# Other homes for the MLP tiles in each partition of SBUF

## The chip, the core and the metric

The kernel runs on one core of a Trainium2 chip. The metric is device time in microseconds, from the start to the end of one execution. Three timed runs of the kernel before gave 779.7, 779.81 and 780.31 us; the median is 779.81 us.

## What is computed

An attention whose mask comes from hashed buckets, on two batches of eight heads with 768 tokens and head size 64, and behind it two MLPs on the 1536 tokens of 512 features that it gives:

```
attn: x[b,h] = softmax(where(bucket(q) == bucket(k), q k^T / 8, -1e9)) v
x = transpose of attn to 1536 x 512
h = x @ w_in  (512 x 2048);  g = h - tanh(h);            x = g @ w_out (2048 x 512)
h = x @ w2_in (512 x 2048);  g = h * sigmoid(1.702 h);   out = g @ w2_out
```

The MLP weights arrive as 64-bit floats.

## The kernel before

**Attention** takes the first 257 us. It walks over 96 steps of 128 queries of one head: scores (line 333), softmax, transposes (line 368), product with v (line 387), and it leaves its result as two fp32r parts, xh (rounded) and xl (the rest).

**The MLPs** follow as 16 chunks, 0 to 7 for the first and 8 to 15 for the second. A chunk is two blocks (j = 0, 1) of 128 hidden features, on three blocks (t) of 512 tokens. Every product is made of three fp32r matmuls, high by high, high by low, low by high. A matmul has a stationary operand, 128 x 128, which LDWEIGHTS loads, and a moving operand, 128 x 512, which MATMUL streams past it; in the profile's names, as in `o<-gh,wh`, the moving one stands first. In line 611 (`products`) the stationary operand is a piece of the w_in weights (wh, wl) or of sums of them (sh, sl), and the moving operand is x (xh, xl) or differences of x (th, tl): sh, sl, th and tl come from a scheme that makes eight block products out of seven. In line 700 (`out_mm`) the first MLP has the w_out weights (wh, wl) stationary and the activations (gh, gl) moving. The second MLP has them the other way round: activations stationary, weights moving. In every steady chunk these are 138 matmuls of 512 columns: 72 in line 700 and 66 in line 611.

The other engines feed that. DVE unpacks the 64-bit weights (raw to w, lines 109 to 135), gates (line 664) and adds outputs to the accumulators acc01 and acc2 (line 708). ACT rounds weights, sums and activations to their high parts (lines 141, 566, 668). POOL makes the low parts (lines 144, 570, 673). The order on every engine is written out by hand in the strings STEADY and ORDER; no scheduler changes it.

**Homes.** A tile pool takes its place in the partition when it is entered, one behind the other, and its tiles lie in it in the order in which they are first asked for. The pools of the attention are closed at line 513, and the MLP's pools are laid over the same bytes. So a tile's home follows from the order of the `tile_pool` calls (lines 75 to 77, 90, 173 to 177, 518 to 522) and from the sizes alone. The first 16 KB of a partition are reserved, four small constants stand behind them, and the first tile starts 128 bytes past 16 KB. All further tiles that matter are multiples of 512 bytes, except `ready`, which has 64 bytes: what lies behind `ready` starts at 192 modulo 512.

Of the kernel before, what the change touches and what calls it, by code (L numbers as in the profile page):

```python
# [10 lines left out]
F32 = mybir.dt.float32  # L11
F32R = mybir.dt.float32r
# [15 lines left out]
NCC = DM // 128  # L28
# [6 lines left out]
TB = 512  # L35
# [22 lines left out]
def lsh_attention_then_two_mlps(  # L58
# [15 lines left out]

    xpool = ctx.enter_context(tc.tile_pool(name="xpool", bufs=1))
    wp0 = ctx.enter_context(tc.tile_pool(name="wp0", bufs=1))
    ps = ctx.enter_context(tc.tile_pool(name="ps", bufs=1, space=PSUM))
    ctx.enter_context(tc.manual_schedule())

    xh = xpool.tile([128, NCC, NT], F32R, name="xh")  # L80
    xl = xpool.tile([128, NCC, NT], F32R, name="xl")

    acc01 = xpool.tile([128, NCC, 2 * TB], F32, name="acc01")

    wh = {}
    wl = {}
    todo = {}
    parts = {}
    wpools = [wp0]
    rawp = [ctx.enter_context(tc.tile_pool(name="rawa", bufs=1))]  # L90

# [422 lines left out]


    wpools.append(ctx.enter_context(tc.tile_pool(name="wp1", bufs=1)))
    rawp.append(ctx.enter_context(tc.tile_pool(name="rawm", bufs=1)))
    op = ctx.enter_context(tc.tile_pool(name="op", bufs=1))  # L520
    sp = ctx.enter_context(tc.tile_pool(name="sp", bufs=2))
    gp = ctx.enter_context(tc.tile_pool(name="gp", bufs=1))
    acc2 = op.tile([128, NCC, TB], F32, name="acc2")
    th = op.tile([128, 3, 2, TB], F32R, name="th")
    tl = op.tile([128, 3, 2, TB], F32R, name="tl")


    ready = op.tile([128, 16], F32, name="ready")
# [9 lines left out]
    gh = {}  # L538
    gl = {}
# [107 lines left out]
    def apart(c, t, j):  # L647
        return t == j or t == 2 if c % LAYER else j == 0
# [15 lines left out]
        nc.vector.tensor_tensor(g, h, f, ALU.subtract if c < LAYER else ALU.mult)  # L664

    def g_hi(c, t, j):
        gh[c, t, j] = gp.tile([128, TB], F32R, tag=f"gh{t}{j}", name=f"gh{c}_{t}_{j}")
        nc.scalar.activation(gh[c, t, j], fs[c, t, j], AF.Copy)  # L668

    def g_lo(c, t, j):  # L670
        gl[c, t, j] = gp.tile([128, TB], F32R, tag=f"gl{t}{j}", name=f"gl{c}_{t}_{j}")
        eng = nc.gpsimd if apart(c, t, j) else nc.vector
        eng.tensor_tensor(  # L673
            gl[c, t, j], fs.pop((c, t, j)), gh[c, t, j].bitcast(F32), ALU.subtract
        )
# [79 lines left out]
    def issue(name, c):  # L755
# [12 lines left out]
        elif kind == "ts":  # L768
            t_sum(c, *n)
        elif kind in ("th", "tl"):  # L770
            (t_hi if kind == "th" else t_lo)(*n)
        elif kind == "P":
            product(c, n[0])
        elif kind in ("kp", "ku"):
            keep(c, n[0], yw[c, 0])
        elif kind in ("xadd", "zadd", "wadd"):
            add(c, kind[0])
        elif kind == "h":
            t, j = n
            tag = "T" if c % LAYER or t != 1 else "vg"[j]  # L780
            hp[c, t, j] = bank(tag, f"h{c}_{t}_{j}")
            h_mm(c, t, j, hp[c, t, j])
        elif kind == "t":
            act(c, *n)
        elif kind == "g":
            gate(c, *n)
        elif kind in ("hi", "lo"):
            (g_hi if kind == "hi" else g_lo)(c, *n)
        elif kind == "o":
            out_mm(c, *n)  # L790
        elif kind == "ev":
            evac(c, *n)
        elif kind in ("xh", "xl"):
            (x_hi if kind == "xh" else x_lo)(*n)
        elif kind == "tab":
            nc.scalar.activation(ready, ready, AF.Sigmoid)
# [136 lines left out]
```

## Time and profile before

| | |
|---|---|
| median of three runs | 779.81 us |
| span of the profiled execution | 778.2 us |
| so, outside the span | 1.6 us |
| TensorE busy (PE) | 759.1 us, 98% |
| VectorE busy (DVE) | 582.0 us, 75% |
| ScalarE busy (ACT) | 424.6 us, 55% |
| GpSimd busy (POOL) | 399.4 us, 51% |
| attention | 0 to 257 us |
| first MLP | 257 to about 522 us |
| second MLP | from there to the end |

The profiled execution was recorded once; its span is what all sums are made against, and 1.6 us are added to come to the median. PE's busy time counts overlapping, modelled ends of pipelined matmuls: a single MATMUL is shown as some 390 ns long while the next one starts 227 to 236 ns after it. What counts for the time is the distance from start to start, called pitch here. At the full clock of 2.4 GHz, 512 columns are 213.3 ns.

### The profile page before, as it was taken

The numbers are of one execution on the slowest core, as the hardware profiler recorded it, in microseconds if no ns is written. First come the engines' busy times: TensorE is split into PE (matmuls) and PEld (weight loads), VectorE is DVE, ScalarE is ACT, GpSimd is POOL, SyncE is SP. The second block draws the span as 40 slices with busy tenths as digits, with TensorE's granted clock in tenths as the row PEclk, the third lists the DMA queues.
The fourth block names the chain that finished last, engine by engine and source line by source line (L and its number), as shares of the span: only waits on it lengthen the run. The fifth ranks groups of instructions, "written<-read, shape, count | busy, mean of one in ns | idle before, by whom it ended". The sixth has DMA issues, their size and how long they took to land.

```text
span 778.2 us, 10045 instructions
## 1 busy us (share of the span) xinstructions
PE 759.1 (98%) x3708; PEld 570.3 (73%) x3708; DVE 582.0 (75%) x840; ACT 424.6 (55%) x793; POOL 399.4 (51%) x342
## 2 busy tenths in 40 slices
PE   4899999999999999999999999999999999999997
PEld 2666666666665788888888888887878888888885
DVE  4778778767766768778787788897798778877643
ACT  3777777777777465454353453556545345353430
POOL 6442651652500686474554735799775473554610
PEclk9999999999999999999999999999999999999999
DMA  9536135134010212021131111212112111120004
GB/s 260 178 102 208 70 103 163 57 107 160 25 54 0 109 55 109 34 76 55 54 109 55 54 55 55 108 27 83 55 55 102 61 55 54 55 109 0 1 1 162
DMA packets 12993, 62.89 MB, mean 81 GB/s; under 512 B 1616, under 2 KB 2512, under 8 KB 8848
## 3 DMA queue, kind: packets, MB, share of 16 engines
q1 hardware_dynamic: 8928, 46.21, 16.4%
q0 software_dynamic: 3872, 15.99, 7.2%
q8 instruction: 29, 0.48, 0.3%
q14 instruction: 20, 0.16, 0.1%
q10 hardware_dynamic: 144, 0.05, 0.0%
HBM read 59.10 MB, written 3.15 MB: 80 GB/s over the span
## 4 chain that ended last, share of the span: by engine, by line
PE 88%; DVE 4%; issue 2%; POOL 2%; DMA 2%; ACT 1%; POOLq 0%; DVEq 0%; ACTq 0%
PE o L700 31%; PE h L611 12%; PE y L611 10%; PE pv L387 9%; PE tp L368 9%; PE sc L333 8%; PE w L611 5%; PE x L611 2%; DMA ka<-in_kd 1%; DMA r<-in_rr 1%; POOL xl L723 1%; DVE nm L347 1%; PE rb L412 1%; PE pb L261 1%; PE po L292 1%
## 5 line engine op out<-in xcount | busy, mean ns | idle before, releaser
L673 POOL TENSOR_TENSOR gl<-f,gh 128x512 fp32r<-128x512 f32 x62 | 85.9, 1386 | 170.9 <-ACT gh L668 165.5
L708 DVE TENSOR_TENSOR acc<-o,acc 128x512 f32<-128x512 f32 x168 | 108.8, 684 | 54.4 <-PE o L700 53.6
L376 ACT ACTIVATE pt<-tp 128x384 f32<-128x384 f32 x184 | 80.3, 489 | 47.7 <-PE tp L368 47.1
L347 DVE TENSOR_REDUCE nm<-sc 128x1 f32<-128x768 f32 x96 | 91.5, 954 | 14.6 <-PE sc L333 13.4
L368 PEld LDWEIGHTS tp<-eye_sb,pr 128*128 128x128 f32 x576 | 61.6, 140 | 53.5 <-issue 25.7
L351 ACT ACTIVATE pr<-sc,nb 128x768 f32<-128x768 f32 x96 | 86.9, 905 | 15.8 <-DVE nb L349 8.8
L144 POOL TENSOR_TENSOR wl<-w,wh 128x512 fp32r<-128x512 f32 (+1 forms) x62 | 85.7, 1393 | 19.0 <-ACT wh L141 19.0
L732 ACT ACTIVATE u<-y 128x512 f32<-128x512 f32 x42 | 25.3, 601 | 107.8 <-PE y L611 107.8
L368 PE MATMUL tp<-eye_sb,pr 128*128 128x128 f32 x576 | 83.5, 281 | 0.0
L387 PE MATMUL pv<-pt,v 128*64 128x384 f32 x384 | 82.0, 510 | 0.0
L700 PE MATMUL o<-wh,gh 128*128 128x512 f32 x192 | 76.2, 397 | 0.7 <-ACT acc L706 0.6
L700 PE MATMUL o<-wh,gl 128*128 128x512 f32 x192 | 76.0, 396 | 0.5 <-POOL gl L673 0.5
L700 PE MATMUL o<-wl,gh 128*128 128x512 f32 x192 | 75.9, 395 | 0.0
L700 PE MATMUL o<-gh,wh 128*128 128x512 f32 x192 | 75.9, 395 | 0.0
L700 PE MATMUL o<-gh,wl 128*128 128x512 f32 x192 | 75.4, 393 | 0.0
L700 PE MATMUL o<-gl,wh 128*128 128x512 f32 x192 | 75.3, 392 | 0.0
L611 PE MATMUL h<-xl,wh 128*128 128x512 f32 x160 | 62.6, 391 | 0.3 <-POOL xl L723 0.3
L611 PE MATMUL h<-xh,wh 128*128 128x512 f32 x160 | 62.6, 391 | 0.0
L611 PE MATMUL h<-xh,wl 128*128 128x512 f32 x160 | 62.6, 391 | 0.0
L333 PE MATMUL sc<-ka,qa 128*128 128x384 f32 x192 | 55.8, 372 | 2.4 <-DVE qa L237 1.9
L668 ACT ACTIVATE gh<-f 128x512 fp32r<-128x512 f32 x62 | 39.0, 629 | 28.3 <-DVE f L664 28.1
L333 PE MATMUL sc<-kb,qb 128*128 128x384 f32 x192 | 50.2, 342 | 2.0 <-DVE qb L299 2.0
(138 smaller groups left out, 1652.1 us busy)
## 6 DMA issues: line engine op xcount, KB each, us to landing
raw<-in_w SPq DMA_DIRECT2D x32, 1024.0 KB, 4.8
ka<-in_kd POOLq DMA_DIRECT2D x7, 768.0 KB, 4.6
qa<-in_qd POOLq DMA_DIRECT2D x7, 768.0 KB, 6.8
r<-in_rr SPq DMA_DIRECT2D x7, 768.0 KB, 4.5
v<-in_vv SPq DMA_DIRECT2D x8, 384.0 KB, 3.1
out<-acc SPq DMA_DIRECT2D x12, 256.0 KB, 2.1
qb<-in_qd POOLq DMA_DIRECT2D x7, 384.0 KB, 8.1
r<-in_rr SPq DMA_DIRECT2D x2, 384.0 KB, 4.5
```

The costliest lines, as they stand in the source:

```text
L144: nc.gpsimd.tensor_tensor(wl[c, j][:, f], ws[c, j][:, f], wh[c, j][:, f].bitcast(F32), ALU.subtract)
L333: nc.tensor.matmul(sc[:, hf, :HALF], (qa, qb)[n][:, h, t0 : t0 + QT], (ka, kb)[n][:, h, hf * HALF : (hf + 1) * HALF], start=(n == 0), stop ...
L347: nc.vector.tensor_reduce(nm, sc[:, :, :HALF], AX.XY, ALU.max, negate=True)
L351: nc.scalar.activation(pr.rearrange("p (a b) -> p a b", a=2), sc[:, :, :HALF], AF.Exp, bias=nb, scale=D**-0.5, accum_out=sums[u][:, j, h : ...
L368: nc.tensor.transpose(tp[:, k * 128 : (k + 1) * 128], pr[:, c * 128 : (c + 1) * 128], eye_sb)
L376: nc.scalar.activation(dst, src, AF.Copy)
L387: nc.tensor.matmul(acc[u][h * 64 : (h + 1) * 64, :UT], v[:, h, c, :], probT[u][:, c, h, :], start=(c == 0), stop=(c == NCH - 1),)
L611: nc.tensor.matmul(o, a, b, start=(start and n == 0 and m == 0), stop=(n == len(pairs) - 1 and m == 2), skip_group_check=not start,)
L668: nc.scalar.activation(gh[c, t, j], fs[c, t, j], AF.Copy)
L673: eng.tensor_tensor(gl[c, t, j], fs.pop((c, t, j)), gh[c, t, j].bitcast(F32), ALU.subtract)
L700: nc.tensor.matmul(o, a, m, start=(first and n == 0), stop=(not first and n == 2))
L708: nc.vector.tensor_tensor(m, o, m, ALU.add)
```

## The change

Seven pools change place; not one instruction is added, removed or moved. On each of the five engines the built programs stand in the same order, instruction for instruction. acc01 goes to a pool of its own (apool) on the right-hand side, that is, at the far end of the partition, and the first block's raw and w buffers (rawa) go there too. th and tl get a pool of their own (tp) directly behind the weights; sh and sl (sp) and gh and gl (new pool ghl) follow, then u and f (gp), then acc2 and `ready` (op), and the second block's raw and w buffers (rawm) come last.

```diff
     xpool = ctx.enter_context(tc.tile_pool(name="xpool", bufs=1))
     wp0 = ctx.enter_context(tc.tile_pool(name="wp0", bufs=1))
+    apool = ctx.enter_context(tc.tile_pool(name="apool", bufs=1, side="right"))
...
-    acc01 = xpool.tile([128, NCC, 2 * TB], F32, name="acc01")
+    acc01 = apool.tile([128, NCC, 2 * TB], F32, name="acc01")
...
-    rawp = [ctx.enter_context(tc.tile_pool(name="rawa", bufs=1))]
+    rawp = [ctx.enter_context(tc.tile_pool(name="rawa", bufs=1, side="right"))]
...
     wpools.append(ctx.enter_context(tc.tile_pool(name="wp1", bufs=1)))
+    tp = ctx.enter_context(tc.tile_pool(name="tp", bufs=1))
+    sp = ctx.enter_context(tc.tile_pool(name="sp", bufs=2))
+    ghl = ctx.enter_context(tc.tile_pool(name="ghl", bufs=1))
+    gp = ctx.enter_context(tc.tile_pool(name="gp", bufs=1))
+    op = ctx.enter_context(tc.tile_pool(name="op", bufs=1))
     rawp.append(ctx.enter_context(tc.tile_pool(name="rawm", bufs=1)))
-    op = ctx.enter_context(tc.tile_pool(name="op", bufs=1))
-    sp = ctx.enter_context(tc.tile_pool(name="sp", bufs=2))
-    gp = ctx.enter_context(tc.tile_pool(name="gp", bufs=1))
+    th = tp.tile([128, 3, 2, TB], F32R, name="th")
+    tl = tp.tile([128, 3, 2, TB], F32R, name="tl")
     acc2 = op.tile([128, NCC, TB], F32, name="acc2")
-    th = op.tile([128, 3, 2, TB], F32R, name="th")
-    tl = op.tile([128, 3, 2, TB], F32R, name="tl")
...
-        gh[c, t, j] = gp.tile([128, TB], F32R, tag=f"gh{t}{j}", name=f"gh{c}_{t}_{j}")
+        gh[c, t, j] = ghl.tile([128, TB], F32R, tag=f"gh{t}{j}", name=f"gh{c}_{t}_{j}")
...
-        gl[c, t, j] = gp.tile([128, TB], F32R, tag=f"gl{t}{j}", name=f"gl{c}_{t}_{j}")
+        gl[c, t, j] = ghl.tile([128, TB], F32R, tag=f"gl{t}{j}", name=f"gl{c}_{t}_{j}")
```

The homes, in KB from the start of a partition, with the start modulo 512 bytes, as the two built programs have them:

| tiles | read by TensorE as | before | after |
|---|---|---|---|
| xh, xl | moving | 16 to 64, 128 | the same |
| wh, wl, even chunks | stationary; moving in the second MLP's line 700 | 80 to 96, 128 | 64 to 80, 128 |
| wh, wl, odd chunks | the same | 108 to 124, 128 | 80 to 96, 128 |
| th, tl | moving | 144 to 168, 128 | 96 to 120, 128 |
| sh, sl | stationary | 168 to 184, 192 | 120 to 136, 128 |
| gh, gl | moving in the first MLP, stationary in the second | 198 to 222, 192 | 136 to 160, 128 |
| u, f | not read | 184 to 198, 192 | 160 to 174, 128 |
| acc2 | not read | 136 to 144, 128 | 174 to 182, 128 |
| raw, w of j = 1 | not read | 124 to 136, 128 | 182 to 194, 192 |
| raw, w of j = 0 | not read | 96 to 108, 128 | 196 to 208, 480 |
| acc01 | not read | 64 to 80, 128 | 208 to 224, 480 |
| attention: qa, qb | stationary | 111 to 135, 128 | 83 to 107, 128 |
| attention: ka, kb | moving | 135 to 159, 128 | 107 to 131, 128 |
| attention: v | stationary | 165 to 171, 128 | 137 to 143, 128 |
| attention: pr | stationary | 171 to 180, 128 | 143 to 152, 128 |
| attention: pt | moving | 180 to 216, 128 | 152 to 188, 128 |

Because the MLP's homes overlap other attention tiles than before, a dozen waits at the seam between attention and MLP differ; all others are the same. The one that starts a transfer later is that of raw1_1, the first load of chunk 1's second block: before, it waits for the last matmul of the attention; after, also for POOL's last piece of the attention (line 436).

## Rows read from the trace of the kernel before

**Rows 1.** The page: busy time by engine, PE's granted clock in 40 slices.
```profile
PE 759.1 (98%) x3708; PEld 570.3 (73%) x3708; DVE 582.0 (75%) x840; ACT 424.6 (55%) x793; POOL 399.4 (51%) x342
...
PEclk9999999999999999999999999999999999999999
```

**Rows 2.** The page: chain of work that ended last, by engine.
```profile
PE 88%; DVE 4%; issue 2%; POOL 2%; DMA 2%; ACT 1%; POOLq 0%; DVEq 0%; ACTq 0%
```

**Rows 3.** PE from 257 us, instructions in order: start us, us, what.
```profile
259.99 0.39 PE L611 MATMUL h<-xh,wh 128*128 128x512 f32 x1
...
267.93 0.39 PE L611 MATMUL h<-xh,wl 128*128 128x512 f32 x1
268.15 0.40 PE L700 MATMUL o<-gh,wh 128*128 128x512 f32 x1
268.39 0.40 PE L700 MATMUL o<-gl,wh 128*128 128x512 f32 x1
```

**Rows 4.** PE in chunk 11 of the second MLP, the same view.
```profile
641.75 0.40 PE L700 MATMUL o<-wh,gh 128*128 128x512 f32 x1
641.99 0.39 PE L700 MATMUL o<-wl,gh 128*128 128x512 f32 x1
...
644.55 0.40 PE L611 MATMUL y<-th,sh 128*128 128x512 f32 x1
```

**Rows 5.** The chain in order of time, merged: start us, us, what xcount.
```profile
366.63 5.51 PE o L700 x24
...
398.42 5.51 PE o L700 x24
...
601.57 5.60 PE o L700 x24
...
633.57 5.60 PE o L700 x24
```

**Rows 6.** PE in the attention at 202 us, scores of 384 columns.
```profile
202.25 0.51 PE L333 MATMUL sc<-ka,qa 128*128 128x384 f32 x2
202.60 0.51 PE L333 MATMUL sc<-kb,qb 128*128 128x384 f32 x2
```

**Rows 7.** The chain in order of time, from 500 to 575 us.
```profile
506.57 1.29 DVE acc L708 x2
...
537.03 1.67 PE o L700 x6
```

**Rows 8.** PE's two longest waits in the MLPs: us in total, times, longest.
```profile
PE o L700 <- ACT acc L706: 0.6, 1, 0.6
PE o L700 <- POOL gl L673: 0.5, 1, 0.5
```

**Rows 9.** One steady chunk: us, busy by engine (instructions), PEclk, DMA share, GB/s.
```profile
602.00:634.00 32.00, 32.00 (x140) 25.93 (x139) 24.83 (x34) 14.16 (x22) 16.79 (x15) 1.00 0.18 66
```

**Rows 10.** Groups by line: busy us, mean ns | idle before, releaser.
```profile
L708 DVE TENSOR_TENSOR acc<-o,acc 128x512 f32<-128x512 f32 x168 | 108.8, 684 | 54.4 <-PE o L700 53.6
...
L368 PE MATMUL tp<-eye_sb,pr 128*128 128x128 f32 x576 | 83.5, 281 | 0.0
L387 PE MATMUL pv<-pt,v 128*64 128x384 f32 x384 | 82.0, 510 | 0.0
...
L126 DVE SCALAR_TENSOR_TENSOR w<-raw,w 128x1024 uint32<-128x1024 uint32 x32 | 42.3, 1322 | 0.4
...
L591 DVE TENSOR_TENSOR acc<-acc 128x512 f32<-128x512 f32 x4 | 6.3, 1568 | 0.8 <-POOL xl L723 0.6 <-issue 0.2
```

**Rows 11.** The seam: SP's queue, POOL and DVE in order of time.
```profile
257.27 0.80 SPq L103 DMA_DIRECT2D raw<-in_w  x2
...
258.50 1.34 POOL L436 TENSOR_TENSOR xl<-xs,xh 128x384 fp32r<-128x384 f32 x1
...
269.43 1.80 DVE L109 TENSOR_SCALAR raw<-raw 128x1024 f32<-128x1024 f32 x1
```

**Rows 12.** The raw tiles from 225 to 300 us: issue to landing.
```profile
DMA to landing us min/median/max: 4.7/4.8/6.8
```

## The prediction, made before the changed kernel had run

> **What bounds the kernel now.** I read the shares of the engines first. TensorE is busy for 98% of the span, and the chain of work that ended last is PE for 88% [rows 1, 2]; its granted clock is 1.00 in every slice, that is, 2.4 GHz. In the MLPs its matmuls waited for other engines for little more than a microsecond in its longest waits [rows 8], and in a steady chunk it is busy for all of 32.00 us while DVE, the next, has 24.8 [rows 9]. So time can come only from the matmuls' own pace, and the next view is the list of matmuls in order of time, from start to start.
>
> There the pace is not one. From 259.99 to 268.15 us, 36 starts of line 611 with xh, xl moving and wh, wl stationary stand 8.16 / 36 = 226.7 ns apart, which is 213.3 ns of columns at 2.4 GHz and 13.3 ns more [rows 3]. The first matmul that streams gh, at 268.15, is 0.24 us long instead of 0.22 or 0.23, on the same weights. In the second MLP 12 matmuls with gh and gl stationary take 641.75 to 644.55, 2.80 / 12 = 233.3 ns each, on the same columns and at the same clock [rows 4]. Nothing waits in between.
>
> What tells the two kinds apart in the table of homes: the quick ones read only tiles between 16 and 124 KB that start at 128 modulo 512; the slow ones read at least one tile that lies between 168 and 222 KB and starts at 192 modulo 512. In before these two marks go together, so the trace can't say which is the cause. The change removes both from everything that TensorE reads in the MLPs.
>
> **The change, part by part.** *The pace.* A steady chunk is 138 matmuls. In the first MLP one chunk lasts from 366.63 to 398.42, 31.79 us or 230.4 ns a matmul; in the second from 601.57 to 633.57, 32.00 us or 231.9 ns [rows 5]. At 226.7 ns a chunk is 31.28 us. That is 0.51 us (1.6%) less in the first MLP and 0.72 us (2.25%) in the second. The first counts from 257 to 506.6 us, where the chain leaves PE [rows 7]: 249.4 x 1.6% = 4.0 us. The second counts from 537.0, where the chain is back on PE [rows 7], to about 770: 233 x 2.25% = 5.2 us. Between 506.6 and 537 the chain runs over DVE, POOL and ACT, which make the second MLP's input; there a quicker PE only waits longer, and I count nothing. For stops of PE that grow when it is quicker I take off 0.3 us, about a quarter of the 1.1 us that rows 8 have now. Sum: 4.0 + 5.2 - 0.3 = 8.9 us.
>
> Is 226.7 ns the right pace for the new homes? Weights at 64 to 96 KB and th, tl at 96 to 120 lie inside the range that is quick now. The activations at 136 to 160 KB and sh, sl up to 136 do not. Their nearest row is the attention: there ka and kb stream from 135 to 159 KB past qa and qb at 111 to 135, all at 128 modulo 512, and two score matmuls of 384 columns take 0.35 us from 202.25 to 202.60, so 175 ns, which is 160 ns of columns and some 15 more [rows 6], the quick kind's surplus. So a moving tile up to 159 KB and a stationary one up to 135 KB cost nothing extra. For a stationary tile from 136 to 160 KB no row stands; its bounds are 0 and the 6.7 ns of rows 4, and I take 0, since it is nearer to 135 KB at the same offset than to 198 KB at another.
>
> The Trainium skill speaks against all this: "TensorE: Matmul & The Clock Gate", section "Wait — 56ns, not 53.3ns?", gives one distance from start to start, columns at 2.4 GHz and about 2.5 ns, 215.7 ns for 512 columns, and no part for the place of an operand. By it the moved tiles would change nothing; rows 3 and 4 differ from it, and by 6.7 ns from each other, so I go by the rows.
>
> *The tiles that move out of the way.* acc01, raw and w go above 182 KB. TensorE does not read them. DVE, ACT, POOL and the DMA do, at 480 or 192 modulo 512 where it was 128. No row shows an operand of theirs at 480. I take 0; the bound on the bad side is the same shape of DVE addition at 1.57 us (line 591) where line 708 takes 0.68 [rows 10]. What hides a small loss is DVE's idle time, 31.3 - 24.8 = 6.5 us in a chunk [rows 9].
>
> *The seam.* raw1_1's load started at 257.27 us; now it also waits for POOL's last piece, which ended at 258.50 + 1.34 = 259.8 [rows 11]. Behind it on SP's queue stands the load of raw2_0, and its first reader is DVE at 269.43, with the gates of chunk 0 queued behind that. Even at 6.8 us to landing [rows 12] it is there at 266.6. I count nothing. If that cover were gone, each microsecond late would hold DVE for as long and PE later for at most that.
>
> *Attention.* Its tiles slide down by 28 KB. Its order, waits and offsets stay. Here v, pr and pt lie above 165 KB now and partly leave that range. The scores are at the quick pace already [rows 6]. For the transposes and the product with v, 576 + 384 matmuls [rows 10], the bounds are 0 and 960 x 6.7 ns = 6.4 us of gain. I take 0: these tiles have been at 128 modulo 512 all along, and their matmuls are shown with 281 / 128 = 2.2 and 510 / 384 = 1.3 ns a column [rows 10] where the MLP's have 0.39 us / 512 = 0.8 [rows 3], so operands are asked for less densely there. A loss has no reason: nothing that TensorE reads there moves up.
>
> **The sum.** 778.2 - 8.9 = 769.3 us of span, and 1.6 outside it: 770.9 us. Between the ends of its own terms (the middle stretch gains 0.5 after all; a quarter of the gain is lost to new stops) this case reaches from 770 to 773.
>
> **Rivals.**
>
> *Part of the new range is still slow.* If a stationary tile at 136 to 160 KB pays 6.7 ns as now, the 72 matmuls of line 700 keep 0.48 of the 0.72 us of each chunk of the second MLP, and of its 5.2 us 1.7 are left: 4.0 + 1.7 - 0.3 = 5.4, so 774.4 us. For it: no row covers that place. Against it: sc's moving operand at up to 159 KB.
>
> *The home is not the cause.* The slow matmuls could be slow because their operands are written shortly before, or for the mix of operands, and wh, wl, xh, xl are older when they are read. Then nothing moves: 779.8 us. Beside it stands the Trainium skill, "SBUF — State Buffer", section "Who interferes with whom": PE never waits on anyone. That fits these rows only if the 6.7 ns come from elsewhere. Against it: xh with wh runs quick in chunk 0, when xh is just as fresh [rows 3], and gh turns the pace at its very first matmul.
>
> *Attention gains too.* All of 6.4 us, of which PE's 88% of the chain counts: 5.6 us more, 765.3 us.
>
> *Slower: DVE at the new offset.* If DVE's work on acc01 (8 of a chunk's 12 additions) took 1.57 us as line 591 did, that is 8 x 0.88 = 7.1 us more in a chunk; if line 126 (2 x 1.32 us a chunk) stretched alike, 3.4 more: 24.8 + 10.5 = 35.3 us, 3.3 above today's 32.0, in some 13 steady chunks 43 us: 823 us. It decides from 7.2 us more on DVE in a chunk. Against it: line 591's rows stand at the seam, beside POOL's waits [rows 10], and may owe their length to that and not to a place.
>
> **Chances.** Forecast 0.72, part of the range slow 0.10, no effect 0.08, attention gains too 0.07, DVE slower 0.03. What a measurement here can tell from no change is 0.2%, 1.6 us. Faster by more than that: 0.72 + 0.10 + 0.07 = 0.89; within it 0.08; slower 0.03. The range of 8 in 10 takes in the forecast's own ends, the case of the part that stays slow, and the lower part of a gain in the attention: 767.5 to 775.0 us.
>
> **What would show it.** Right: 12 matmuls of line 700 in either MLP take 2.72 us, steady chunks are 31.28 us long in both, the attention still ends at 257 us, additions of line 708 stay at 0.68 us, and the stretch between the MLPs is as long as before. Wrong: line 700 still at 2.80 in the second MLP alone (part of the range), or in both (no effect); new waits of PE on line 708 or 673; a seam that begins with DVE waiting for raw.

## The result, and the profile after

The changed kernel takes 771.84 us (median of 4 runs, 771.06 to 772.15) where the one before takes 779.99 (4 runs, 779.7 to 780.31): 0.9893 of the time, 95% interval 0.9881 to 0.9905, so 1.07% faster. The prediction was 770.9 us, range 767.5 to 775.0. The span of the profiled execution went from 778.2 to 770.0 us.

The page of after, busy time by engine and granted clock, beside [rows 1]; then the chain of work by engine, beside [rows 2]:

```profile
PE 749.5 (97%) x3708; PEld 570.0 (74%) x3708; DVE 585.1 (76%) x840; ACT 424.3 (55%) x793; POOL 400.6 (52%) x342
...
PEclk9999999999999999999999999999999999999999
...
PE 88%; DVE 3%; POOL 2%; issue 2%; DMA 2%; ACT 1%; POOLq 0%; DVEq 0%; ACTq 0%
```

The same work, the same clock (granted 1.000 and 0.999 on the mean), the same bound; PE is busy 9.6 us less. The chain in order of time, merged (start us, us, what), shows where, beside [rows 5] and [rows 7]:

```profile
364.93 5.44 PE o L703 x24
...
396.21 3.85 PE o L703 x17
...
502.63 1.29 DVE acc L711 x2
...
533.07 1.66 PE o L703 x6
...
588.15 5.44 PE o L703 x24
...
619.43 5.44 PE o L703 x24
```

A steady chunk is 396.21 - 364.93 = 31.28 us in the first MLP (31.79 before) and 619.43 - 588.15 = 31.28 in the second (32.00 before). That is 226.7 ns a matmul in both. The chain leaves PE at 502.63 instead of 506.57 and is back at 533.07 instead of 537.03, so the stretch between the MLPs is 30.44 us where it was 30.46.

PE in the second MLP, instructions in order of time, beside [rows 4]: the same 12 matmuls of `out_mm`, from 635.59 to 638.31, take 2.72 us where they took 2.80. The last row is the last matmul of the kernel:

```profile
635.59 0.39 PE L703 MATMUL o<-wh,gh 128*128 128x512 f32 x1
635.82 0.39 PE L703 MATMUL o<-wl,gh 128*128 128x512 f32 x1
...
638.31 0.39 PE L614 MATMUL y<-th,sh 128*128 128x512 f32 x1
...
764.33 0.39 PE L703 MATMUL o<-wh,gl 128*128 128x512 f32 x1
```

In before the last matmul starts here (same view):

```profile
773.37 0.39 PE L700 MATMUL o<-wh,gl 128*128 128x512 f32 x1
```

So up to the last matmul 773.37 - 764.33 = 9.04 us are gained, but the span is only 8.2 us shorter. The rest is lost behind the last matmul, where the last outputs are stored: 778.2 - 773.37 = 4.83 us before, 770.0 - 764.33 = 5.69 (from the unrounded times) after.

### The profile page after: what moved, and what is told of

Its sections match the earlier page's. It is cut to its first block, busy times and chain, and to the rows that moved or that the text cites. A ratio compares the mean times of both kernels' runs of the same rounds, so it can differ in the third digit from the quotient of the medians.

```text
span 770.0 us, 10036 instructions
## 1 busy us (share of the span) xinstructions
PE 749.5 (97%) x3708; PEld 570.0 (74%) x3708; DVE 585.1 (76%) x840; ACT 424.3 (55%) x793; POOL 400.6 (52%) x342
## 4 chain that ended last, share of the span: by engine, by line
PE 88%; DVE 3%; POOL 2%; issue 2%; DMA 2%; ACT 1%; POOLq 0%; DVEq 0%; ACTq 0%
PE o L703 31%; PE h L614 12%; PE y L614 10%; PE pv L388 10%; PE tp L369 9%; PE sc L334 8%; PE w L614 5%; PE x L614 2%; DMA r<-in_rr 1%; DMA ka<-in_kd 1%; POOL xl L726 1%; PE rb L413 1%; PE pb L262 1%; PE po L293 1%; DVE acc L594 1%
```

## The experiments

All times are medians of 4 to 10 runs, each kernel beside the kernel before on the same chip, which had 780.06 to 780.40 us. Two columns of the table are worked out from PE's rows: *surplus* is what the start-to-start distances of the MLPs' matmuls (2204 of them, in two kernels one or two fewer; the 15 to 17 stops above 245 ns are left out) exceed 226.67 ns (8.16 / 36) by, summed; 226.7 below is that pace, rounded. *24 of out_mm* is the length of such a piece of the chain in the first and second MLP.

| kernel | start modulo 512 of what TensorE reads in the MLPs | us | ratio to before, interval | 24 of out_mm, us | surplus, us |
|---|---|---|---|---|---|
| before | x, w, th, tl 128; sh, sl, gh, gl 192 | 779.99 | | 5.51, 5.60 | 9.74 |
| after | all 128 | 771.84 | 0.9893 (0.9881 to 0.9905) | 5.44, 5.44 | 0.24 |
| e1_offset_only | all 128, places of before | 771.26 | 0.9882 (0.9868 to 0.9897) | 5.44, 5.44 | 0.30 |
| e2_low_192 | as before, places of after | 781.11 | 1.0009 (1.0000 to 1.0019) | 5.51, 5.60 | 9.74 |
| e3_acc2_low | all 128 | 771.29 | 0.9884 (0.9869 to 0.9898) | 5.44, 5.44 | 0.32 |
| e4_all_0 | all 0 | 770.67 | 0.9876 (0.9862 to 0.9891) | 5.44, 5.44 | 0.33 |
| e5_moved_256 | 128; sh, sl, gh, gl 256 | 780.43 | 1.0003 (0.9993 to 1.0012) | 5.57, 5.59 | 10.30 |
| e6_moved_160 | 128; sh, sl, gh, gl 160 | 781.21 | 1.0018 (1.0009 to 1.0027) | 5.60, 5.59 | 10.89 |
| e7_all_192 | all 192 | 771.19 | 0.9885 (0.9868 to 0.9901) | 5.44, 5.44 | 0.35 |
| e8_low_parts_192 | high parts 128, low parts 192 | 780.41 | 0.9998 (0.9988 to 1.0007) | 5.55, 5.57 | 10.72 |
| e9_low_192_order | the same, other order of the three matmuls | 780.12 | 0.9999 (0.9989 to 1.0008) | 5.55, 5.55 | 9.87 |
| e10_moved_384 | 128; sh, sl, gh, gl 384 | 771.03 | 0.9881 (0.9867 to 0.9896) | 5.44, 5.44 | 0.37 |
| e11_attention_64 | all 128; the attention mixes 128 and 192 | 770.94 | 0.9879 (0.9864 to 0.9894) | 5.44, 5.44 | 0.29 |
| e12_sp_seven_more | as after | 771.85 | 0.9893 (0.9876 to 0.9909) | 5.44, 5.44 | 0.32 |

### Place or offset

The prediction had two marks on the slow tiles, a place above 168 KB and a start at 192 modulo 512, and could not tell them apart. Two edits do. In e1 the tiles stay where they were in before, moved up by 448 bytes; in e2 they stay where after has them, moved up by 64 bytes.

```diff
 e1, in before:
     ready = op.tile([128, 16], F32, name="ready")
+    pad = op.tile([128, 112], F32, name="pad")
 e2, in after:
+    padp = ctx.enter_context(tc.tile_pool(name="padp", bufs=1))
     sp = ctx.enter_context(tc.tile_pool(name="sp", bufs=2))
...
+    pad = padp.tile([128, 16], F32, name="pad")
```

> The kernel before with 448 unused bytes behind `ready`: sh, sl, gh, gl, u and f keep their high homes (168.6 to 222.6 KB) and begin at 128 modulo 512 instead of 192. Nothing else moves. Theory A (the place above 168 KB is the cause): as before, 780.0 us, 12 matmuls of line 700 in the second MLP take 2.80 us, steady chunks 31.8 and 32.0 us. Theory B (the start modulo 512 is the cause): as after, 771.8 us, 2.72 us, 31.28 us in both MLPs. Both at once (each half of it): about 776 us.

> The kernel after with 64 unused bytes ahead of sh: sh, sl, gh and gl stay low (120 to 160 KB) and begin at 192 modulo 512 instead of 128 (u, f and acc2 too, raw and w of j = 1 at 256). Theory A (place above 168 KB): as after, 771.8 us, 12 matmuls of line 700 in 2.72 us, chunks 31.28 us. Theory B (start modulo 512): as before, 780 us, 2.80 us, 31.8 and 32.0 us, the low homes notwithstanding.

The chain of e1, with gh and gl at 198.6 to 222.6 KB:

```profile
365.15 5.44 PE o L701 x24
...
396.43 5.44 PE o L701 x24
...
596.61 5.44 PE o L701 x24
...
627.89 5.44 PE o L701 x24
```

and of e2, with gh and gl at 136 to 160 KB:

```profile
366.37 5.51 PE o L705 x24
...
601.34 5.60 PE o L705 x24
```

e1 has chunks of 31.28 us in both MLPs (396.43 - 365.15, 627.89 - 596.61) at the old places; e2 has the old 5.51 and 5.60 us at the new places, and its surplus is that of before to the hundredth. So of the two marks the place counts for nothing, and the starts modulo 512 make the difference. One line of 448 unused bytes brings the whole gain of the seven pools.

### Which starts are good

Then which? Three theories were left: a start must be a multiple of 128 bytes (C); the stationary and the moving operand must start alike (D); nearer to 0 is better (E). Four kernels, and later a fifth (e10), differ from before only in two numbers of unused bytes:

```diff
+    pad0 = xpool.tile([128, A // 4], F32, name="pad0")   # ahead of xh
     xh = xpool.tile([128, NCC, NT], F32R, name="xh")
...
     ready = op.tile([128, 16], F32, name="ready")
+    pad = op.tile([128, B // 4], F32, name="pad")
# e4: A 384, B 448    e5: no A, B 64    e6: no A, B 480    e7: A 64, B 448    e10: no A, B 192
```

> The kernel before with 384 unused bytes ahead of xh and 448 behind `ready`: every tile that TensorE reads, in the attention too, begins at 0 modulo 512, in the order of before (gh, gl at 199 to 223 KB). Theory C (a tile that TensorE reads must begin at a multiple of 128 bytes): as e1_offset_only, 771.3 us, pitch 226.7 ns, 2.72 us for 12 matmuls of line 700. Theory D (stationary and moving operand must begin alike modulo 512): the same 771.3 us. Theory E (0 is better than 128): below 770 us, a pitch under 226 ns.

> The kernel before with 64 unused bytes behind `ready`: sh, sl, gh, gl (and u, f) begin at 256 modulo 512, all else that TensorE reads at 128. Theory C (multiples of 128 bytes): 771.3 us, 2.72 us for 12 matmuls of line 700 in the second MLP. Theory D (both operands alike modulo 512): about 780 us, 2.80 us.

> The kernel before with 480 unused bytes behind `ready`: sh, sl, gh, gl (and u, f) begin at 160 modulo 512, 32 bytes past a multiple of 128. Theory C (multiples of 128) and theory D (both alike modulo 512): about 780 us, 2.80 us for 12 matmuls. If the cost grows with the distance from a multiple of 128, about 776 us and 2.76 us. If only 64 bytes past counts, or if it is multiples of 32 that are good: 771.3 us, 2.72 us.

> The kernel before with 64 unused bytes ahead of xh and 448 behind `ready`: every tile that TensorE reads begins at 192 modulo 512, in the attention too. Theory C (multiples of 128 bytes): every matmul of the MLPs pays, 2208 x 6.7 ns = 14.7 us where before pays 9.7, so 785 us, and up to 6.4 us more in the attention, 791 us. Theory D (both operands alike modulo 512): 771.3 us, pitch 226.7 ns.

C fell twice: e5 is slow though 256 and 128 are multiples of 128, and e7 is quick though nothing is. The chain of e5, then that of e7:

```profile
367.52 5.57 PE o L701 x24
...
602.97 5.59 PE o L701 x24
```

```profile
364.78 5.44 PE o L702 x24
...
596.26 5.44 PE o L702 x24
```

E falls too: e4's matmuls have the same pace as those of e1. D stands: at 0, 128 and 192 alike, the pace is quick when both start the same. Differences of 32, 64 and 128 bytes all cost about the same (10.89, 9.74 and 10.30 us). e10 asks for the difference of 256:

> The kernel before with 192 unused bytes behind `ready`: sh, sl, gh, gl (and u, f) begin at 384 modulo 512, all else that TensorE reads at 128, so they are 256 bytes apart. If the starts must be alike modulo 512: about 780 us, 2.80 us for 12 matmuls of line 700 in the second MLP, like e5_moved_256, where they are 128 apart. If alike modulo 256 is enough: 771.3 us, 2.72 us.

```profile
364.51 5.44 PE o L701 x24
...
595.92 5.44 PE o L701 x24
```

This chain is quick. So it is enough here that the starts are alike modulo 256 bytes; modulo 512 isn't needed.

### Alike with what

In every slow kernel so far the operands of one matmul differ, and so do the moving operand and the weights that LDWEIGHTS reads for the next matmul while it streams (in e8's trace a stream starts at 600.125 us and that LDWEIGHTS at 600.128). e8 takes the second kind of difference away and leaves the first. In both kernels the low parts go to pools of their own at 192 modulo 512; e9 then exchanges two matmuls.

```diff
 e8:
+    padp = ctx.enter_context(tc.tile_pool(name="padp", bufs=1, side="right"))   # 288 bytes
+    lp0 = ctx.enter_context(tc.tile_pool(name="lp0", bufs=1, side="right"))     # xl, wl of even chunks
...
+    lpools.append(ctx.enter_context(tc.tile_pool(name="lp1", bufs=1, side="right")))   # wl of odd chunks, tl, gl
+    lps = ctx.enter_context(tc.tile_pool(name="lps", bufs=2, side="right"))            # sl
...
+    pad = op.tile([128, 112], F32, name="pad")
 e9, besides:
-            for m, (a, b) in enumerate(((ah, bh), (ah, bl), (al, bh))):
+            for m, (a, b) in enumerate(((ah, bh), (al, bh), (ah, bl))):
...                                                      (and the same in out_mm)
```

> All low parts (xl, wl, tl, sl, gl) begin at 192 modulo 512 (in pools at the far end of the partition), all high parts (xh, wh, th, sh, gh) at 128; the order of the instructions is before's. The three matmuls of a product are, stationary by moving, high by high, high by low, low by high. So of the three, two have operands that begin differently; but while each of them streams, the LDWEIGHTS of the next one reads a tile that begins as the streamed one does: high streams, high is loaded; low streams, low is loaded; high streams, high is loaded. Theory D1 (stationary and moving operand of one matmul must begin alike): two of three matmuls pay 6.7 ns, 1472 x 6.7 = 9.9 us over e1_offset_only, about 781 us. Theory D2 (what the next LDWEIGHTS reads must begin like what streams beside it): nothing pays, 771.3 us. Theory F (two starts in one kernel are enough): about 780 us.

> As e8_low_parts_192, the same homes, but with the second and third matmul of each product exchanged: high by high, low by high, high by low. Still two of three have operands that begin differently. But now, while high streams, low is loaded; while high streams, high is loaded; while low streams, high is loaded: two of three loads begin otherwise than the stream beside them. D1: as e8_low_parts_192, about 781 us. D2: two of three pay, 1472 x 6.7 ns = 9.9 us, about 781 us, where e8_low_parts_192 has 771.3. F: about 780 us.

The chain of e8, then that of e9, from one long piece to that of the next chunk:

```profile
602.39 5.57 PE o L707 x24
...
634.44 5.57 PE o L707 x24
```

```profile
601.98 5.55 PE o L707 x24
...
633.87 5.55 PE o L707 x24
```

D2 falls: e8 is as slow as before though what is loaded always starts like what streams. Its chunk is 634.44 - 602.39 = 32.05 us. e9's is 31.89 us, 231.1 ns a matmul, just what D1 asks for: 226.7 + 2/3 x 6.7 = 231.1. D1 also sizes all the slow kernels by nearly one price. Before, e2, e5 and e6 have 1152 matmuls of out_mm and 336 with sh or sl whose operands differ, 1488; e8 and e9 have two thirds of 2219, 1479. The surpluses divided by these are 6.5 (before, e2), 6.9 (e5), 7.3 (e6), 7.2 (e8) and 6.7 ns (e9).

That price is a share of the total, not the cost of one matmul. In e9 the distances after the three matmuls of a product are 231.7 (high by high, alike), 233.3 (low stationary) and 228.4 (low moving) ns on the mean, so the cost does not stand at just the matmuls whose operands differ. In before the same 64 bytes cost 5.51 / 24 = 229.6 ns a matmul in the first MLP and 5.60 / 24 = 233.3 in the second, where the two operands have exchanged their starts; at 128 and 32 bytes (e5, e6) both MLPs pay nearly the same. And the matmuls of x with wh and wl, whose operands are alike, have up to 230 ns on the mean in before. PE in order of time there, from the last matmul with sl (unlike) into those with wh and wl (alike):

```profile
360.73 0.39 PE L611 MATMUL y<-th,sl 128*128 128x512 f32 x1
360.96 0.39 PE L611 MATMUL h<-xh,wh 128*128 128x512 f32 x1
...
362.35 0.39 PE L611 MATMUL h<-xh,wh 128*128 128x512 f32 x1
...
364.16 0.39 PE L611 MATMUL y<-xh,wl 128*128 128x512 f32 x1
```

The first six distances between alike operands, 360.96 to 362.35, are 1.39 / 6 = 232 ns; the next eight, 362.35 to 364.16, are 1.81 / 8 = 226 ns, as quick as [rows 3]. In after, where all operands are alike, the same uneven pace stands behind every stop, at the start of the MLPs for instance:

```profile
257.51 0.40 PE L614 MATMUL h<-xl,wh 128*128 128x512 f32 x1
...
259.59 0.39 PE L614 MATMUL h<-xl,wh 128*128 128x512 f32 x1
...
260.27 0.39 PE L614 MATMUL h<-xl,wh 128*128 128x512 f32 x1
```

Nine distances of 2.08 / 9 = 231 ns, then 226 to 227. So the slow pace is not the property of unlike operands alone: alike ones have it too for some four to ten matmuls behind a stop or behind unlike ones, and then settle at 226.7; unlike ones stay slower for as long as they last. What settles was not tried.

F, that two starts in one kernel are enough, is not told apart from D1 by e8 and e9. Against it stand chunk 0, where 36 matmuls with operands alike ran at 226.7 ns in before too [rows 3], and e11 below, whose attention mixes two starts while its MLPs keep the quick pace (surplus 0.29). That streams which change their start from one matmul to the next add to the cost in e8 is not excluded; it can't be the cost in before, where within `out_mm` all streams start alike. How the starts of two operands come to cost time stays open.

### The attention

> e1_offset_only (MLP tiles all at 128) with 2 x 32 unused bytes ahead of ka in the attention: ka, kb, r, v, pr and pt begin at 192 modulo 512, qa, qb, the mask's tables and eye stay at 128. So scores (ka moving, qa stationary) and transposes (eye moving, pr stationary) mix two starts, the product with v (pt moving, v stationary) doesn't. If the attention's matmuls pay as the MLPs' do: up to 5 ns for each of 384 columns and 1.7 ns for each of 128, or 6.7 ns for any, that is 1 to 6 us on PE, of which only the part that PE's chain has in the attention shows: 771.5 to 775 us. If its matmuls ask too thinly for operands to notice: 771.3 us, attention over at 257 us.

```diff
+            (i or n != "ka" or qk.tile([128, 8], F32, name="pada")) and
             qk.tile([128, 2, S], F32R, tag=n, name=f"{n}{i}") for n in ("qa", "qb", "ka", "kb")
```

Scores and transposes mix two starts here. In its trace two scores still stand 0.35 us apart (201.86 to 202.21), as in [rows 6], and the first matmul of the MLP starts at 256.61, no later than the 257.17 of after:

```profile
201.86 0.51 PE L334 MATMUL sc<-ka,qa 128*128 128x384 f32 x2
202.21 0.50 PE L334 MATMUL sc<-kb,qb 128*128 128x384 f32 x2
...
256.61 0.50 PE L613 MATMUL h<-xh,wh 128*128 128x512 f32 x1
```

At 770.94 us the attention doesn't notice. The scores ask for their operands as densely as the MLPs do (0.35 / 2 = 175 ns for 384 columns, 0.46 ns each, where the MLPs have 226.7 / 512 = 0.44), so a thinner demand is not why they escape. Why they do (four in a row only, shorter streams, or another reason) was not tried.

### The end of the kernel

> The kernel after with acc2 moved from 174 to 182 KB to 96 to 104 KB (128 modulo 512 in both); th, tl, sh, sl, gh, gl, u and f go up by 8 KB, so gh and gl end at 168 KB. After's end, from the last matmul's start to the end of the span, is 5.69 us where before's was 4.83. If acc2's home, which the last stores read, makes that: 4.8 us and 771.0 us. If not (the state of the DMA queues in that one execution): any of 4.8 to 5.7 us in the profile, and 771.8 us, as after. For both theories of the pace: 2.72 us for 12 matmuls of line 700, since gh and gl still lie under 168 KB at 128 modulo 512.

```diff
+    a2p = ctx.enter_context(tc.tile_pool(name="a2p", bufs=1))
     tp = ctx.enter_context(tc.tile_pool(name="tp", bufs=1))
...
-    acc2 = op.tile([128, NCC, TB], F32, name="acc2")
+    acc2 = a2p.tile([128, NCC, TB], F32, name="acc2")
```

e3's end is 5.47 us, so acc2's place is not what makes after's end longer. Its median, 771.29, is nearer to the 771.0 forecast for the other outcome, but not by the end: in its trace the first matmul of the MLPs starts at 256.31 us, where after's starts at 257.17. The DMA view of the last 6.2 us (40 slices) shows more. Here is e1, whose end takes 4.83 us:

```profile
GB/s 0 0 0 0 0 0 0 0 0 0 0 0 145 410 383 383 397 383 357 383 396 331 370 383 396 397 383 357 396 383 133 0 0 0 0 0 0 0 0 0
...
q1 hardware_dynamic: 576, 1.05, 45.1%
...
out<-acc SPq DMA_DIRECT2D x4, 256.0 KB, 2.1
```

and here after:

```profile
GB/s 0 0 0 0 0 0 0 251 396 330 370 397 436 383 330 344 344 370 383 383 278 132 370 410 396 344 66 26 26 26 26 0 0 0 0 0 0 0 0 0
...
q1 hardware_dynamic: 576, 1.05, 45.5%
q14 instruction: 1, 0.01, 0.8%
...
out<-acc SPq DMA_DIRECT2D x4, 256.0 KB, 2.9
```

In after one packet of the instruction queue, 8 KB, lies among the last stores, 1.4 us behind the last matmul's start; it took 0.81 us. From then on it looks as if one of the 16 DMA engines were late: the stores end with four slices at 26 GB/s, a sixteenth of 410, some 0.6 us long. The view doesn't name the engine. In all ten traces with an end of 4.8 us (before, e1, e4 to e11) that packet lies about 17 us ahead of the last matmul; in after, e2, e3 and e12, with ends of 5.5 to 5.7 us, at 1.3 to 1.4 us behind it. That e2 is 0.7 us slower than before (781.11 and 780.40), with the same surplus, fits this. e12 tried to move it by the length of SP's program:

> The kernel after with seven stores of 8 bytes, DRAM to an unused tile, added to SP's queue behind the load of chunk 4's second block, at a time when SP has nothing else to do; homes and all other engines as in after. SP's program has 137 instructions again as in before, where after has 130. In after, e2_low_192 and e3_acc2_low an 8 KB packet of the instruction queue lies 1.3 to 1.4 us behind the last matmul's start, among the last stores, and from that start to the end of the span it is 5.5 to 5.7 us; in all kernels with 137 it lies some 17 us ahead of the last matmul, and the end takes 4.8 us. If SP's code fetch makes the difference: the packet at -17 us, an end of 4.8 to 4.9 us, and a median 0.5 to 0.9 us under after's 771.84, so 771.0 to 771.3. If the homes of after make it (acc01, raw and w above 182 KB): the end stays at 5.7 us, and the median at 771.8, wherever the packet lies.

```diff
+        if (c, j) == (4, 1):
+            dum = rp.tile([128, 16], F32, name="dum")
+            for k in range(7):
+                nc.sync.dma_start(out=dum[0:1, 2 * k : 2 * k + 2], in_=eye[0:1, 2 * k : 2 * k + 2])
```

```profile
GB/s 0 0 0 0 0 0 0 0 291 410 330 383 436 370 370 370 304 370 383 423 423 225 304 370 383 396 172 27 26 26 26 0 0 0 0 0 0 0 0 0
...
q14 instruction: 1, 0.01, 0.8%
```

The packet stayed at 1.4 us and the end at 5.59 us, so the length of SP's program is not it, and this run can't tell the packet from the homes. Two things fit all fourteen traces. The four with the late packet are just those built on after's order of pools, and in just these four POOL's program is shorter (459 records, 460 or 461 in the other ten), because a wait at the seam went away. Neither was tried by itself. What is shown is that the late packet and the longer end go together, and that the end is 0.6 to 0.9 us longer with it.

## Why the prediction was right, point by point

**The bound and the pace.** Right. Every class of matmul in the MLPs is at 226.4 to 227.1 ns in after, and the gain came from there and from nowhere else. One reading behind it was too simple: that what reads only tiles at 128 is quick in before. On the mean of the MLPs the matmuls with wh and wl in line 611 stood 227.5 to 229.9 ns apart there, many of them close behind slow ones. The sum didn't suffer, since it went by whole chunks.

**First MLP, 4.0 us.** Measured 506.57 - 502.63 = 3.94. **Second MLP with the stops, 5.2 - 0.3 = 4.9.** From the chain's return to PE to the last matmul: 773.37 - 537.03 = 236.34 before, 764.33 - 533.07 = 231.26 after, so 5.08. **The middle stretch, nothing.** 30.46 and 30.44. PE's wait for ACT there grew as said; PE's longest waits in the MLPs in after, beside [rows 8]:

```profile
PE o L703 <- ACT acc L709: 0.7, 1, 0.7
PE h L614 <- POOL xl L726: 0.6, 1, 0.6
PE o L703 <- POOL gl L676: 0.5, 1, 0.5
```

The 15 stops hold 3.94 us above the pace where they held 3.54, so 0.4 against the 0.3 taken off. In sum 9.04 us up to the last matmul against 8.9.

**The seam.** Right. raw1_1's load starts at 260.32 behind POOL's last piece (258.96 + 1.33), 3.05 us later than before, and DVE reads the next load at 269.07 without a wait, beside [rows 11] (SP's queue, POOL, DVE):

```profile
260.32 0.80 SPq L104 DMA_DIRECT2D raw<-in_w  x2
...
258.96 1.33 POOL L437 TENSOR_TENSOR xl<-xs,xh 128x384 fp32r<-128x384 f32 x1
...
269.07 1.78 DVE L110 TENSOR_SCALAR raw<-raw 128x1024 f32<-128x1024 f32 x1
```

**The tiles that move out of the way.** Right. Groups by line (busy us, mean ns), beside [rows 10]: acc01 at 480 modulo 512 leaves the addition at 684 ns and the unpacking at 1329 where it was 1322. The four forms of line 591 went from 20.6 to 21.5 us together, off the chunk's path.

```profile
L711 DVE TENSOR_TENSOR acc<-o,acc 128x512 f32<-128x512 f32 x168 | 108.6, 684 | 48.6 <-PE o L703 48.1
L127 DVE SCALAR_TENSOR_TENSOR w<-raw,w 128x1024 uint32<-128x1024 uint32 x32 | 42.5, 1329 | 0.4
```

**The new homes.** Right that they cost nothing, but partly by luck. The row that it leaned on, two scores in 0.35 us, can't show a price: in e11 scores with unlike starts take the same 0.35. What settled it was the start, and that was alike.

**Attention.** Right that it gains nothing: the first matmul of the MLP starts at 257.17 after 257.12 (before's unrounded record; 256.3 to 258.0 in the fourteen traces). Its reason, that operands are asked for less densely, was read for the transposes and the product with v from shown lengths, whose ends are modelled, and was not tested; for the scores, as e11 shows, it is not needed.

**The end and the base: the misses.** No step of the prediction looked behind the last matmul; there 0.86 us were lost, as shown above. And the 1.6 us outside the span were the difference of a median and of another execution's span; the four executions of after have 2.1 to 2.2 each, as has before where its span and time are of one execution (779.96 and 777.8 us). So of the 0.94 us between 770.9 and 771.84, the end is +0.86, the base +0.55 and the MLPs -0.14; the median lies 0.31 below the profiled execution, and these add up to 0.96, which is the 0.94 within rounding.

**The rivals.** *Part of the range slow*: fell, and for a reason that the prediction didn't have. It argued that 136 to 160 KB is near to 135 KB; e1 shows that even 198 to 223 KB is not slow. The other half of its sentence, "at the same offset", carried the result. *The home is not the cause*: fell as a forecast, yet half of it is right: the home as such is not the cause, and the mix of operands, which that rival named, is, if mix means how they start. *Attention gains* and *DVE slower*: fell.

Two rules can be set against this. The Trainium skill, "TensorE: Matmul & The Clock Gate", section "Wait — 56ns, not 53.3ns?", has one distance for 512 columns, 215.7 ns, and no term for the operands' starts; here, with fp32r operands, it is 226.7 ns with like starts and up to 233.3 with unlike ones. The Trainium skill, "SBUF — State Buffer", section "Who interferes with whom", calls TensorE's two reads, of the moving operand and of the weights, independent; the table above shows that the starts of the two together change the pace, though not whether the reads themselves get in each other's way. On the distance the measurements differ, and they decide; on the ports no run here can tell.

## What to carry to other kernels

Where PE is the bound, list the distances from start to start by pair of operands before looking for waits; if like matmuls have two paces, compare the starts of their tiles modulo 256 bytes, and make those of the stationary and of the moving operand the same (shown here for fp32r matmuls of 512 columns). A slow distance need not stand at its cause: the matmuls behind can pay. A single small tile, such as the 64 bytes of `ready`, shifts all tiles behind it in its partition; here 448 bytes behind it did alone what seven moved pools did. When two marks go together in the trace, as place and offset did, change one at a time: the change was right, but for half of its stated reason.

## What the runs showed that was not expected

- Where stationary and moving operands start 32, 64 or 128 bytes apart, the MLPs lose 9.74 to 10.89 us, 6.5 to 7.3 ns for each such matmul of 512 columns; starts 256 apart, and those alike at 0, 128 or 192 modulo 512, cost next to nothing (surplus 0.24 to 0.37 us over 2204 distances).
- Alike matmuls pay as well for some four to ten starts behind a stop or behind unlike ones (231 or 232 ns), before they settle at 226.7.
- Where the tiles that TensorE reads lie (16 to 223 KB), and whether they start at 0, 128 or 192, has no effect by itself.
- An 8 KB packet of the instruction queue among the last stores goes with an end that is 0.6 to 0.9 us longer; what puts it there is open.
